# Another order of the steps in the six plans of an attention, gating and rotation kernel

## The chip, the core and the metric

The kernel runs on one core of one Trainium2 chip. The core has five engines with a queue each: TensorE (PE; its weight loads are shown as PEld), VectorE (DVE), ScalarE (ACT), GpSimd (POOL) and SyncE (SP, which only issues transfers). The metric is the device time of one execution in microseconds, and the number that stands for a kernel is the median of its runs.

## The reference

Three parts follow each other, all in fp32, for 8 batches of 576 positions: linear attention over 8 heads of 64, a gated block with a product over the positions, and a rotation block with two products over the positions.

```python
# attention: q, k, v are (8, 8, 576, 64)
q_s = softmax(q, axis=-1);  k_s = softmax(k, axis=2)
kv = np.einsum('bhsd,bhse->bhde', k_s, v)
x = heads_side_by_side(np.einsum('bhsd,bhde->bhse', q_s, kv))   # (8, 576, 512)
# gated block
h = np.maximum(x @ w_in, 0.0)                     # (8, 576, 1024)
u, v = h[..., :512], h[..., 512:]
v_n = (v - mean(v)) / np.sqrt(var(v) + 1e-06)
v_s = np.einsum('ts,bsd->btd', w_spatial, v_n) + b_spatial[None, :, None]
x = (u * v_s) @ w_out
# rotation block
theta = x @ w_theta
y = np.einsum('ts,bsd->btd', w_tok_r, x * np.cos(theta)) \
  + np.einsum('ts,bsd->btd', w_tok_i, x * np.sin(theta))
u = x + y
return u + np.maximum(u @ w_ch, 0.0)
```

## The kernel before

Every number is held as a high and a low part, and every product is three matmuls (high by high, high by low, low by high), so TensorE has most of the work. The kernel has two phases. Phase 1 goes through the batches and does the attention and the gated block; its results are written to DRAM. Phase 2 goes through the batches again and does the rotation block. The products over the positions in phase 2 are done with combined weights (seven products Q0 to Q6 for each batch, line 850), whose parts are made in phase 1.

The order of the work is written out by hand. A plan is a string of words; each word is one step (a function of some instructions), and the words are emitted from left to right within a manual schedule. Each engine issues its own instructions in the order of their emission and waits where an operand or a buffer isn't ready; between engines there is no order but that. So a plan sets the order on each queue, SP's and POOL's transfers among them, and which of the buffers in rotation a step gets. PSUM has three tiles of two banks and two of one bank in phase 1, two and four in phase 2; nine tiles of 128x576 ("t2") rotate in SBUF.

There are six plans. PLANS[0] (batch 0), PLANS[1] (batch 1), PLAN (batches 2 to 6) and LAST (batch 7) make phase 1; PLAN2 (batches 0 to 6) and LAST2 (batch 7) make phase 2. A word has a name, a number, flags (v: on VectorE, p: on GpSimd, c: on ScalarE; a, b: a part of the heads), and a stroke for work on the batch before.

- Attention, for the batch that comes next: ldk, ldq, ldv load (SP). kmax (VectorE, lines 373 to 381), kt (TensorE transposes, 388), kr (394), kbc (402), kmb (ScalarE, 407), ksub, kexp make the softmax of k, and K (446) the product with v, kn (459 to 467) its norm. qmax, qsub, qexp, qsum (501), qmul (509) make that of q; T (514) and t (525 to 528) turn it, X and x (528, 546) make the input of the gated block.
- Gated block: U (TensorE, line 187) and r (relu on ScalarE, 614); V (line 195), v (statistics, 567 to 578) and N (norm, 586 to 600); S (the product over positions, 187) and G (the gate, 629 on VectorE, 630 on ScalarE, 631 on VectorE or GpSimd); Y (187) and y (copy on ScalarE, 645, and a store).
- The weights come as 64-bit words and are converted on chip, 35 pieces in a fixed order, one for each pair of words B (first half: 242 to 264) and P (second half: 280 to 284); E makes sums for phase 2 (326 to 358). Plan 0 converts 18 pieces of w_in, w_sp and w_out while it runs the first batch.
- Phase 2, for the batch at hand: Q0 to Q6, with a (874), e (874), d (861), h (863), l (865) and s1, s4 operands late (f, F, g, G: 881, 883) between them; b loads the next operand (GpSimd, 674); C (line 195 or 187's helper) and o (905) make the output; in the last batch x does this by halves (917).
- Phase 2, for the batch that comes next: j, J (the input's high and low part, 687, 689), R (the remainder's parts, 707 and 708), m (theta, 195), w (730), t (737 to 742), r (749), y (757), z (764 to 772), s (787, 788), n (793, 794), p (798 to 802), i (807, 809), k (814, 817), I (821) and L (824). In LAST these stand with an H ahead of the word.

Of the kernel before, what the change touches and what calls it, by code (L numbers as in the profile page):

```python
# [1195 lines left out]
```

## Time and profile before

| | us |
|---|---|
| median of 3 runs | 1011.98 |
| lowest and highest | 1011.37 and 1012.64 |
| profiled execution | 1012.96 |
| its span in the trace | 1011.2 |
| TensorE busy | 948.7 |
| VectorE busy | 778.4 |
| ScalarE, GpSimd busy | 484.3 and 496.1 |

The profile's rows are of one execution. In a timeline row stand the start, the length, the engine, the line, the operation, the tiles written and read, the number of instructions, and in brackets the idle time before it with what ended it. The order of the rows on one engine is its order of issue. Phase 1 takes the first 587 us and phase 2 the rest; plan 0 takes the first 130, in which TensorE's granted clock is below full.

### The profile page before, as it was taken

To read this page: it belongs to the slowest core of one execution; us is meant where nothing else is said; L and a number is where in the kernel's file an instruction comes from. 1 tells how busy PE (TensorE), PEld (TensorE's weight loads), DVE (VectorE), ACT (ScalarE), POOL (GpSimd) and SP (SyncE) were. 2 spreads that over 40 slices of the span, in tenths; PEclk is the share of its full clock that TensorE was granted. 3 is DMA by queue.
4 is the path that set the end of the run, shared out by engine and by line. 5 is a ranking of instruction groups with operands and counts; after the bars stand their busy time and mean duration, and the time that the engine had idled before them with its cause. 6 is when DMAs were issued, how large, how long until landed. Compare 5 with 4: busy or idle time off the path is not lost.

```text
span 1011.2 us, 17199 instructions
## 1 busy us (share of the span) xinstructions
PE 948.7 (94%) x6816; PEld 893.8 (88%) x6816; DVE 778.4 (77%) x1140; ACT 484.3 (48%) x828; POOL 496.1 (49%) x496
## 2 busy tenths in 40 slices
PE   3588898999999999999999989999999999999997
PEld 2467888999899999999989989999999899999997
DVE  7887867877878778787424878988797988887863
ACT  3745446553555545545434645445353545454520
POOL 6366147554646566535202344646382637464460
PEclk9888899999999999999999999999999999999999
DMA  8542240516535365340132484544444262614332
GB/s 292 191 130 87 100 191 11 194 58 204 176 108 193 117 218 171 119 168 15 54 140 84 152 304 141 188 141 155 148 175 147 96 240 86 243 71 174 143 129 94
DMA packets 48064, 147.87 MB, mean 146 GB/s; under 512 B 8304, under 2 KB 21872, under 8 KB 38768
## 3 DMA queue, kind: packets, MB, share of 16 engines
q1 hardware_dynamic: 40464, 92.16, 26.0%
q0 software_dynamic: 7520, 54.63, 15.3%
q8 instruction: 53, 0.87, 0.4%
q14 instruction: 27, 0.22, 0.1%
HBM read 113.38 MB, written 33.39 MB: 145 GB/s over the span
## 4 chain that ended last, share of the span: by engine, by line
PE 46%; DVE 7%; POOL 5%; issue 2%; ACT 2%; DMA 1%; DVEq 0%; POOLq 0%; ACTq 0%
PE ps L850 18%; PE ps L187 14%; PE pb L195 9%; PE ps L195 3%; PE pb L757 1%; DVE t L787 1%; POOL s L793 1%; POOL w L807 1%; POOL s L794 1%; POOL w L814 1%; DVE t L764 1%; DVE w L814 1%; DVE t L741 1%; DVE t L765 1%; DMA sp<-op_w 1%
## 5 line engine op out<-in xcount | busy, mean ns | idle before, releaser
L187 PE MATMUL ps<-sp,vn 128*128 128x288 f32 x896 | 131.9, 306 | 9.6 <-DVE t L629 4.7
L187 PEld LDWEIGHTS ps<-sp,vn 128*128 128x128 f32 x896 | 125.5, 196 | 11.6 <-DVE t L629 4.9
L187 PE MATMUL ps<-g,wo 128*128 128x288 f32 x768 | 106.9, 297 | 1.7 <-ACT t L645 1.7
L187 PEld LDWEIGHTS ps<-g,wo 128*128 128x128 f32 x768 | 103.1, 189 | 2.8 <-ACT t L645 2.8
L187 PE MATMUL ps<-xh,w 128*128 128x288 f32 x512 | 95.1, 303 | 9.3 <-ACT w L280 7.7
L195 PE MATMUL ps<-w,xh 128*128 128x512 f32 x320 | 97.3, 397 | 3.4 <-ACT t L567 2.9
L187 PEld LDWEIGHTS ps<-xh,w 128*128 128x128 f32 x512 | 78.6, 193 | 11.3 <-ACT w L280 7.9
L187 PE MATMUL ps<-uh,wo 128*128 128x288 f32 x448 | 80.8, 296 | 0.0
L195 PE MATMUL pb<-w,xh 128*128 128x512 f32 x256 | 80.3, 395 | 0.0
L195 PEld LDWEIGHTS ps<-w,xh 128*128 128x128 f32 x320 | 59.2, 188 | 17.2 <-ACT t L567 3.5
L187 PEld LDWEIGHTS ps<-uh,wo 128*128 128x128 f32 x448 | 66.8, 188 | 0.9
L850 PE MATMUL ps<-sp,vn 128*128 128x288 f32 x360 | 60.4, 302 | 6.2 <-DVE t L772 4.0
L850 PEld LDWEIGHTS ps<-sp,vn 128*128 128x128 f32 x360 | 51.8, 192 | 7.8 <-ACT vn L802 4.2
L187 PE MATMUL ps<-xl,w 128*128 128x288 f32 x256 | 56.0, 301 | 0.0
L793 POOL TENSOR_TENSOR s<-t,t 128x256 f32<-128x256 f32 x30 | 23.8, 793 | 64.2 <-DVE t L788 64.2
L195 PEld LDWEIGHTS pb<-w,xh 128*128 128x128 f32 x256 | 46.8, 188 | 9.5
L730 ACT ACTIVATE t<-pb 128x512 f32<-128x512 f32 x36 | 21.5, 598 | 69.0 <-PE pb L195 57.9
L630 ACT CAST g<-t 128x576 fp32r<-128x576 f32 x32 | 21.5, 673 | 67.6 <-DVE t L629 67.5
L850 PE MATMUL ps<-sp,s 128*128 128x288 f32 x384 | 53.7, 295 | 0.0
L850 PEld LDWEIGHTS ps<-sp,s 128*128 128x128 f32 x384 | 52.4, 188 | 0.6
L850 PE MATMUL ps<-sp,w 128*128 128x288 f32 x288 | 48.9, 302 | 3.8 <-DVE w L814 3.3
L631 POOL TENSOR_TENSOR g<-t,g 128x576 fp32r<-128x576 f32 x17 | 25.2, 1485 | 52.2 <-ACT g L630 52.2
(251 smaller groups left out, 2502.2 us busy)
## 6 DMA issues: line engine op xcount, KB each, us to landing
sp<-op_t POOLq DMA_DIRECT2D x24, 1152.0 KB, 5.7
sp<-op_w POOLq DMA_DIRECT2D x16, 1152.0 KB, 5.4
vb<-in_v SPq DMA_DIRECT2D x8, 1300.0 KB, 7.6
y<-t SPq DMA_DIRECT2D x32, 288.0 KB, 2.2
qb<-in_q SPq DMA_DIRECT2D x7, 1152.0 KB, 5.5
out<-t SPq DMA_DIRECT2D x28, 288.0 KB, 2.2
kb<-in_k SPq DMA_DIRECT2D x6, 1152.0 KB, 5.1
st<-in_w_tok SPq DMA_DIRECT2D x9, 576.0 KB, 3.9
```

Source lines behind the costliest of these rows:

```text
L187: nc.tensor.matmul(out=ps[:, c, 0:CH], lhsT=a, rhs=w[:, c * CH:(c + 1) * CH], start=first and i == 0, stop=final and i == last,)
L195: nc.tensor.matmul(out=ps, lhsT=a, rhs=w, start=(i == 0), stop=(i == last))
L630: nc.scalar.copy(out=g_s[m], in_=g)
L631: eng.tensor_tensor(out=g_s[4 + m], in0=g, in1=f(g_s[m]), op=ALU.subtract)
L730: nc.scalar.activation(out=w, in_=ps, func=ACTF.Copy, scale=INV_2PI, bias=MAGIC)
L741: nc.vector.scalar_tensor_tensor(out=r, in0=w, scalar=-TWO_PI_LO, in1=r, op0=ALU.mult, op1=ALU.add)
L757: nc.tensor.transpose(yn[:, j * P:(j + 1) * P], y, ident)
L764: nc.vector.tensor_tensor(out=r, in0=r, in1=yn, op=ALU.mult)
L765: nc.vector.tensor_tensor(out=w, in0=w, in1=yn, op=ALU.mult)
L793: eng.tensor_tensor(out=th["s4"][:, t, :], in0=r[:, LO], in1=x, op=ALU.subtract)
L814: eng.tensor_tensor(out=z[1], in0=w, in1=f(z[0]), op=ALU.subtract)
L850: nc.tensor.matmul(out=ps[:, m, 0:CH], lhsT=a, rhs=x, start=i == 0, stop=i == len(pairs) - 1)
```

## The change

All six plans get another order of their words. Each plan keeps the same words with the same flags, so that each engine has the same instructions as before; nothing else in the kernel is changed. The words of B and P take the pieces in the same order as before, and each piece has its halves on the same engine.

```diff
--- before.py
+++ after.py
@@ -31,49 +31,50 @@
 ORDER = "u1 u0 u2 v3 u3 v2 v1 v0 s0 s3 s5 s2 s4 s1 o0 o2 o1 o3"
 LOADS = "ldk1 ldq1 ldv1 ldw2 ldw4"
 PLAN = (
-        "B0p V2 v2 qexp1 qsum1 qmul1 V1 v1 V0 v0 V4 v4 N2 N0 K1 kn1 U0 V3 r0 v3 N4v U2 r2 ldk2 N3cv N1 "
-        "U3 r3 P0 U1 r1 E0 T0 B t0 E1 S0 X0 G0 T1 P0v t1 S1 T2 S2 x0 kmax2 kt2 ldv2 t2 X1 G1 T3 ldq2 E0 "
-        "G2v x1 S3 kr2 G3v E1 kbc2 kmb2 Y0 t3p qmax2 y0 X2 x2 B0 Y1 qsub2 Y2 y1 X3 y2 Y3 ksub2v P0 x3 "
-        "kexp2 y3 E0v E1 "
-    )
+    "V1 V2 V4 v1 qexp1 V0 B0p K1 qsum1 qmul1 U2 V3 v2 v4 v0 U3 kn1 N0 N2 U0 v3 r2 U1 N4v N3cv "
+    "T0 r3 N1 r0 S0 r1 ldk2 P0 E0 T1 B t0 G0 X0 S1 T2 x0 E1 t1 kmax2 t2 S2 kt2 ldv2 G1 T3 P0v "
+    "G2v kr2 X1 x1 ldq2 E0 t3p S3 G3v kbc2 X2 E1 Y0 qmax2 Y1 y0 x2 y1 qsub2 kmb2 Y2 B0 ksub2v "
+    "y2 P0 X3 Y3 x3 y3 kexp2 E0v E1 "
+)
 PLANS = {
     0: (
-        "kmax1' kt1' kr1' kbc1' kmb1' qmax1a' qsub1a' qmax1b' qsub1bv' qexp1a' qexp1b' ksub1b' ksub1av' "
-        "qsum1a' qmul1a' kexp1a' K1a' kexp1b' K1b' qsum1b' ldk2' B0s' B0s' kn1a' qmul1b' T1' T2' T0' P' "
-        "t0' t1p' kn1b' T3' t2p' X0' x0' ldq1 t3' X1' x1' P' X2' X3' x2' x3' B U0 B0 ldv1 P0v P0v U1 r1 "
-        "B B B0p P0v U3 r0 B0 B0ps P0v P0 P0v B0s B0s kmax1 B0 P0 V0 kt1 v0 P0v U2 P V1 V4 kr1 r2 qmax1 "
-        "qsub1v B0 P N0cv B0p P P v1 kbc1 kmb1 ksub1 N1v V3 v3 v4 V2 v2 qexp1 N3 N2 N4 B0s qsum1 qmul1 "
-        "S1 kexp1 S0 G0 B0 G1 K1 kn1 B ldk2 S2 ldv2 G2 r3 kmax2 T0 t0 S3 kt2 P0v P G3v T1 t1p kr2 P0v "
-        "Y0 y0 X0 x0 T2 t2 kbc2 Y1 y1 B P0v T3 X2 Y2 X1 ldq2 x2 kmb2 y2 Y3 ksub2v t3 X3 x1p x3 qmax2 "
-        "qsub2 y3 "
+        "kmax1' qmax1a' kt1' qsub1a' kr1' qexp1a' kbc1' kmb1' qmax1b' qsub1bv' ksub1b' qexp1b' "
+        "qsum1a' qmul1a' ksub1av' qsum1b' kexp1a' K1a' qmul1b' kexp1b' T3' B0s' T1' B0s' K1b' T0' "
+        "kn1a' P' T2' t0' t1p' kn1b' t2p' X0' x0' t3' ldk2' X1' x1' X2' B B0 X3' P' x3' P0v x2' B "
+        "P0v P0v B U3 B0p B0 U0 P0v P0 r3 P0v U1 V0 r1 r0 kmax1 ldq1 B0ps P0 v0 qmax1 U2 V1 B0s "
+        "ldv1 P0v B0s N0cv V4 r2 B0 B0 V3 qsub1v P B0p P V2 v1 P P v4 v3 N1v kt1 v2 qexp1 N3 kr1 "
+        "N2 N4 kbc1 kmb1 qsum1 S0 ksub1 B0s S1 S2 kexp1 K1 qmul1 G0 T0 B0 G1 G2 kn1 T1 t0 ldk2 "
+        "kmax2 P0v S3 ldv2 B P G3v P0v kt2 t1p kr2 Y0 y0 X0 T2 x0 t2 Y1 X2 kbc2 B x2 X1 y1 T3 t3 "
+        "P0v kmb2 ksub2v Y2 ldq2 Y3 qmax2 y2 x1p X3 y3 qsub2 x3 "
     ),
     1: (
-        "V0 v0 kexp1 N0v V1 v1 V2 K1 qexp1 V3 kn1 v2 qsum1 qmul1 ldk2 U0 r0 V4 v3 U1 v4 r1 U2 T0 U3 B "
-        "N1 N2 N3 N4 t0p S0 r2 r3 B0p G0 T1 t1 ldv2 X0 S1 x0 X1 T2 G1 t2p kmax2 x1p S2 T3 ldq2 t3p kt2 "
-        "kr2 P E0 E1 P0v E0 E1 S3 X2 G2 G3v x2p kbc2 Y0 y0 B0s qmax2 Y1 Y2 y1 kmb2 P0v E0 E1 ksub2v "
-        "qsub2 y2 Y3 y3 X3 x3 kexp2 "
+        "V1 kexp1 V0 v1 V2 U1 v0 qexp1 v2 V4 N1 V3 qsum1 qmul1 K1 r1 N2 v4 U0 v3 kn1 r0 ldk2 B "
+        "N0v T0 t0p N4 U3 N3 r3 U2 ldv2 r2 S0 T1 X0 B0p P S1 G0 E0 x0 t1 kmax2 X1 S2 G1 x1p T2 T3 "
+        "kt2 ldq2 S3 t2p kr2 E1 X2 t3p G2 X3 G3v P0v Y0 qmax2 kbc2 Y2 x2p x3 Y1 y0 kmb2 E0 E1 y1 "
+        "y2 B0s qsub2 Y3 y3 ksub2v P0v kexp2 E0 E1 "
     ),
 }
 PLAN2 = (
-    "L1' L3' y4' Q0 f1 n3' f0 i2' I2v' R i3' I3' b0 z4' s4' p4' k4' I1' c j0 a0 Q1 Q2 j2 j1 J2 j3 "
-    "J3 b1 ldc f3 e0 g2 G2v g1 g3 G1v i4c' d0 y0 J1 f2 y1 h0 Q3 g0 G0v J0 m0 w0 G3 F3v e1 a2v Q4 t0 "
-    "r0 F0v m1 w1 e2 F2v F1 a1 z0 d1 l0v b2 a3v h1 t1c r1 s0 ldr Q5 d2 h2 l2v b3 n0 Q6 b4 d3 l1 m2 "
-    "n4' z1 s1 h3 l3 p0 k0p m3 L0p w2 t2c L4p' w3 t3c i1 C0 o0 i0c p1 k1p r2 C1 r3 y2 y3 C2 m4 I0 "
-    "o1 n1 z2 s2 C3 n2 z3 s3 p2 k2p o2 L2p w4 t4 o3 ldy p3 I4' r4 k3 "
+    "Q0 i2' L3' I1' i3' c y4' b0 I3' I2v' L1' f0 Q1 z4' p4' j1 k4' a0 j3 J1 Q2 e0 y0 n3' d0 "
+    "f2 g1 b1 j0 y1 g2 g0 G2v g3 R G1v Q3 n4' J3 b2 j2 J2 f3 J0 G3 h0 G0v m0 e1 a2v s4' ldc "
+    "w0 a1 t0 F2v m1 f1 w1 Q4 t1c a3v Q5 r1 e2 F1 l0v r0 F3v F0v d1 z0 s0 z1 Q6 h1 d2 m2 b3 "
+    "m3 l1 d3 p0 h3 h2 i4c' n0 y3 w2 s1 l3 p1 l2v L0p i0c y2 ldr t2c k0p n1 w3 b4 t3c C0 m4 "
+    "r2 C1 r3 o0 I0 C2 z2 s2 k1p o1 p2 z3 s3 p3 o2 C3 k3 n2 w4 t4 r4 k2p i1 o3 ldy L4p' L2p "
+    "I4' "
 )
 LAST2 = (
-    "L1' L3' y4' Q0 f1 n3' f0 i2' I2v' i3' I3' b0 z4' s4' p4' k4' I1' c a0 Q1 Q2 b1 f3 e0 g2 G2v g1 "
-    "g3 G1v i4c' d0 f2 h0 Q3 g0 G0v G3 F3v e1 a2v Q4 F0v e2 F2v F1 a1 d1 l0vv b2 a3v h1 Q5 d2 h2 "
-    "l2vv b3 Q6 b4 d3 l1v n4' h3 l3v L4p' I4' x0 x1 x2 x3 x4 x5 x6 x7 "
+    "i4c' I1' L1' i3' i2' Q0 I4' b0 L4p' f2 f1 s4' I3' L3' c Q1 a0 n3' I2v' y4' b1 f3 g1 G1v "
+    "f0 Q2 g3 G3 Q3 F2v e0 F0v F1 d0 g0 F3v h0 b2 l0vv k4' g2 G2v G0v e1 a2v Q4 e2 a1 d1 a3v "
+    "p4' Q5 Q6 d2 h1 z4' h2 l2vv d3 h3 l3v x2 l1v b3 x3 x1 x6 b4 x7 x0 x5 x4 n4' "
 )
 LAST = (
-        "ldy0 V2 v2 V0 v0 U1 N2v r1 V1 v1 N1v N0c V4 V3 v3 th U0 ldr v4 N4 B0 P0v B0s E0 E1v P E0 E1v "
-        "U2 r2 U3 ysp0 ysp1 N3c r3 B0p P0v ysp3 S0 ysp2 r0 S1 G0 Hm0 G1v Hy1 Hm1 Hw1 Ht1c Hw0 Ht0c S2 "
-        "rsp G2v Hr0 S3 ldy1 G3v Hm2 Hw2 Hm3 Hr1 E0 E1 Ht2 Hr2 Hy0 Hz0 Hs0 Hn0v Hp0 Hm4 Hy3 tok HL0 Hz1 "
-        "Hw3 Hs1 Y0 y0 Ht3 Hy2 Hz2 Hi0c Y2 Y3 Hk0p HI0v Hn1v Hp1 Hi1c Hk1p Hr3 Hw4 y2 HL1p Hs2 Hn2 Ht4c "
-        "Hp2 Hi2 Hr4 y3 HL2 Hz3 Y1 y1 Hs3 Hk2 HI2 Hy4 Hz4 Hn3 Hp3 HL3 Hs4 Hn4 Hi4 HI4v Hp4 HL4p Hi3 Hk3 "
-        "HI3v HI1v Hk4 "
-    )
+    "V0 V2 v2 V1 P0v v0 N2v V4 E0 N0c v1 E1v v4 V3 U1 v3 N4 ldy0 r1 N3c U2 N1v U0 S1 U3 r0 P "
+    "E0 G1v ldr B0 ysp2 th ysp1 S0 ysp3 rsp ysp0 Hm0 G0 Hw0 r2 E1v Hm1 Hm2 Ht0c Hw1 Hy0 S2 "
+    "Ht1c Hr0 S3 Hw2 Hy1 r3 Hy2 Hz0 Ht2 P0v Hm3 Hs0 Hr1 Hn0v Hr2 G2v G3v Hi0c Hp0 Hz1 Hk0p "
+    "Hw3 B0s Hm4 Hs1 Ht3 Hp1 E0 HI4v Hn1v HL1p Hz2 Hi4 Y0 Hi1c Hs2 HI1v Hr3 B0p Hp2 E1 Hw4 "
+    "tok Y2 ldy1 Hs4 Hi2 Hn2 Hy3 y0 HL0 Y1 HI0v Y3 Hy4 Hz3 Hs3 Ht4c Hp3 HI2 Hn4 y2 HL2 Hk2 "
+    "Hk3 Hr4 Hi3 Hn3 HL3 Hz4 Hp4 Hk4 y3 HL4p HI3v y1 Hk1p "
+)
 
 
 OPS = ("w11", "t2", "w21", "t3", "t1", "t4", "w22")
```

## Rows read from the trace of the kernel before

**Rows 1.** The page's first part, busy time of each engine, share, instructions.

```profile
PE 948.7 (94%) x6816; PEld 893.8 (88%) x6816; DVE 778.4 (77%) x1140; ACT 484.3 (48%) x828; POOL 496.1 (49%) x496
```

**Rows 2.** Busy time by stretch: length, PE PEld DVE ACT POOL, PEclk, DMA share, GB/s.

```profile
100.00:125.00 25.00, 20.34 (x137) 20.32 (x137) 21.31 (x34) 11.80 (x21) 5.65 (x4) 0.86 0.28 102
...
300.00:400.00 100.00, 97.80 (x730) 91.71 (x731) 81.32 (x111) 53.02 (x82) 59.10 (x52) 1.00 0.53 186
```

**Rows 3.** TensorE's waits by line: us in total, times, longest.

```profile
PE pb L388 <- DVE t L381: 10.7, 3, 7.8
PE ps L187 <- ACT w L280: 7.7, 1, 7.7
...
PE ps L187 <- DVE t L629: 4.7, 1, 4.7
PE ps L850 <- DVE t L772: 4.0, 1, 4.0
PE ps L850 <- DVE w L814: 3.3, 3, 1.1
...
PE ps L195 <- ACT t L567: 2.9, 2, 1.5
...
PE ps L187 <- ACT t L645: 1.7, 3, 0.8
PE ps L514 <- DVE qt L528: 1.6, 1, 1.6
PE ps L187 <- ACT u L614: 1.4, 3, 0.7
PE ps L850 <- DMA sp<-op_w: 1.2, 1, 1.2
...
PE ps L850 <- DVE kb L861: 0.8, 1, 0.8
```

**Rows 4.** Timeline of TensorE in plan 0: start, us, instruction, idle before.

```profile
50.27 0.85 PE L187 MATMUL ps<-xh,w 128*128 128x288 f32 x2 [7.69 <-ACT w L280]
...
76.05 0.73 PE L195 MATMUL ps<-w,xh 128*128 128x512 f32 x2 [1.39 <-ACT t L567]
...
104.69 6.69 PE L187 MATMUL ps<-sp,vn 128*128 128x288 f32 x28 [4.66 <-DVE t L629]
```

**Rows 5.** Timeline of TensorE in plan 2, its step Y3.

```profile
256.13 3.45 PE L187 MATMUL ps<-g,wo 128*128 128x288 f32 x24 [0.76 <-ACT t L645]
```

**Rows 6.** Timeline of DVE from 85 us: G2's start and kmax2.

```profile
103.88 0.75 DVE L629 TENSOR_TENSOR t<-ps,u 128x576 f32<-128x576 f32 x1
104.55 0.68 DVE L373 TENSOR_TENSOR t<-kb 128x512 f32<-128x512 f32 x1
105.27 1.99 DVE L376 TENSOR_TENSOR t<-t,kb 64x256 f32<-64x256 f32 x2
107.29 1.42 DVE L381 TENSOR_TENSOR t<-t,kb 128x512 f32<-128x512 f32 x2
```

**Rows 7.** The page's DMA issues, KB each, us to landing.

```profile
kb<-in_k SPq DMA_DIRECT2D x6, 1152.0 KB, 5.1
```

**Rows 8.** Line 284 on DVE: ns least, median, most; first and last start.

```profile
L284 DVE TENSOR_TENSOR st<-t,t x7: 692/759/1659, 178.5 to 486.7; 128x512 fp32r<-128x512 f32 x4, 128x576 fp32r<-128x576 f32 x3
```

**Rows 9.** Timeline of TensorE in phase 2, the border of a batch.

```profile
699.31 0.40 PE L850 MATMUL ps<-sp,w 128*128 128x288 f32 x1 [1.12 <-DVE w L814]
```

**Rows 10.** Timeline of DVE at the same border.

```profile
698.58 0.68 DVE L814 TENSOR_TENSOR w<-t,w 128x512 fp32r<-128x512 f32 x1
```

**Rows 11.** Line 708 (R's subtraction) on DVE: ns least, median, most.

```profile
L708 DVE TENSOR_TENSOR kvl<-yr,kvh x4: 684/3336/3358, 558.5 to 862.5; 128x512 fp32r<-128x512 f32 x4
```

**Rows 12.** Timeline of GpSimd in the last batch: a1 and b2.

```profile
982.76 2.00 POOL L874 TENSOR_TENSOR t<-t,kb 128x576 f32<-128x576 f32 x1 [6.71 <-DVE t L874]
984.71 0.57 POOL L674 DMA_DIRECT2D sp<-op_w  x1
```

**Rows 13.** Timeline of TensorE in the last batch: Q6.

```profile
990.29 1.04 PE L850 MATMUL ps<-sp,vn 128*128 128x288 f32 x6 [1.22 <-DMA sp<-op_w]
```

## The prediction

> **What bounds the kernel now.** I read the page's busy line first [rows 1]: TensorE is busy for 948.7 of 1011.2 us, so at most about 62 us can be won by any order, and only where TensorE stands still or runs on a low clock. The second view is busy time by stretch [rows 2]: in the 25 us from 100 on TensorE works 20.34 us at a granted clock of 0.86, while in the 100 us from 300 on it works 97.80 at clock 1.00. So plan 0 (all up to 130 us) has idle time and a half-clock part; the later plans have almost none. The third view is TensorE's waits by line [rows 3]. The reader is to see that the long ones happen once (7.8, 7.7, 4.7, 4.0 us), each in plan 0 or at the border of the phases, and that the short ones, up to 1.1 us, come at the borders of steps in the later plans. The engines issue in the order in which the plans' words are emitted, and nothing fixes the order of one engine against another. So a new order does two things only: it changes which instruction stands behind which on one queue, and when a buffer comes free.
>
> The profiled execution took 1012.96 us, 1.76 more than its span of 1011.2; the median of the runs is 1011.98, 0.98 below it. I make the sum on the span and carry its difference to the median. About 0.2%, 2.0 us, is what a measurement of this kernel can tell from no change.
>
> **Plan 0.** The instructions are the same, so only waits are added or removed.
>
> First products. Before, U0 and U1 run early, then TensorE waits 7.7 us for a converted piece of w_in, and U3 starts at 50.27 us [rows 4]. In the new order U3 comes first and needs the fifth converted piece; x3' and x2' (the last parts of x for batch 0) stand behind two more conversions on DVE. Counting DVE's instructions up to x2', I estimate the start of U3 at 46.5 us. The stretch before it gets emptier, so I take U3's 24 matmuls at the cold price. The row at 104.69 [rows 4] gives 6.69/28 = 0.239 us per matmul in a stretch where the clock is low; the row of a Y step on the warm clock [rows 5] gives 3.45/24 = 0.144, with its latency in it. U3 then ends at 52.2, U0 and U1 take 24 x 0.133 = 3.2 each (an estimate for back-to-back running, a little below the 0.144), and V0 starts near 58.6, against 50.27 + 24 x 0.239 = 56.0 before: +2.6 us.
>
> The Trainium skill (TensorE: Matmul & The Clock Gate, What's actually happening) says that the clock falls to 1.2 GHz after idling and comes back to 2.4 GHz only under sustained work. The rows agree in that the granted clock is below 1.00 just in the stretch with the waits [rows 2]; by the rule U0 would be cold too, and the plan 2.5 us longer than in my sum. The sum doesn't use it.
>
> V products. Before, V0 U2 V1 V4 V3 V2 have kt1 and kbc1 between them and stop for 2.9 us in two places for v statistics [rows 3]; the second stop ends at 76.05 [rows 4], from which V2 still has some 2.9 us to go, so it ends near 79. In the new order kt1 and kbc1 stand behind V2, and v0 and v1 have r1, r0 ahead of them but more products to hide behind. Five 12-matmul pieces of V, and U2, back to back need 16.4 us from 58.6, which gives 75.0; with some of the old cold stretch left I take 76. V2 ends 3 us earlier (0 to 4). The v chain up to S0 is the same in both and moves along.
>
> S3 and the second half. Before, S3 waits 4.7 us for G2 [rows 3], whose first instruction is issued at 103.88 [rows 6], behind kn1 and a whole conversion (B) on DVE. In the new order G2 stands directly behind G1, ahead of kn1 and that B: this wait goes, -4.7. What is late next is kmax2. It needs ldk2, which needs K1 to release kb; the landing takes 5.1 us [rows 7] and kmax2 0.68 + 1.99 + 1.42 = 4.1 [rows 6]. So kt2 can run 9.3 us behind K1. TensorE has T0, T1 and S3 between them (0.54 + 0.54 + 3.7 = 4.8, estimates at 0.133 per matmul for S3's 28) and waits about 4.7. G3v now stands behind kmax2 and a conversion's P0v, so Y0's last quarter is late by about 0.7 more. Before, kt2's wait cost about 1.4 (10.7 less the 7.8 at the very start, shared by two) [rows 3]. Net: +4.7 + 0.7 - 1.4 = +4.0. Bounds: +1 if ldk2 lands sooner than the row, +7 if G3v makes all of Y0 wait.
>
> Plan 0 in sum: -3.0 - 4.7 + 4.0 = -3.7, between -9 and +2.
>
> **Plans 1 to 6.** The rows give 1.7 us on y's copy (L645), 1.6 on qt (L528) and 1.4 on U's relu (L614) [rows 3]. In the new PLAN y1 stands before kmb2 and B0 on ACT and the r steps are spread, so 3.1 us go; of the 1.6 in plan 1 I keep half, a gain of 0.8. Against this, P0v now stands between G1 and G2v on DVE in five plans. Its multiplication alone takes 0.76 us at the median and up to 1.66 [rows 8], and S3 needs the PSUM tile that G reads. G2v's lateness is hidden by T3 and X1 in part; I take 0.2 us each, 1.0 in sum (0 to 7). Net -2.9, between -4 and +4.
>
> **LAST.** The head products still start when Hz4 is done, and the 4.0 us wait on L772 [rows 3] stays. Y1 waits about 1 for y0, which stands behind Hp2 and Hw4 on ACT; the gain of U before S balances it. Net 0, between -1 and +2.
>
> **PLAN2, seven batches.** Before, k3 (the low part, L814) is issued last of a batch, behind o3, and o3 waits for C3. At a batch's border Q0 therefore waits, as at 699.31 for 1.12 us [rows 9], where DVE does L814 only at 698.58, after o3 [rows 10]. In the list this is 3.3 us in three places [rows 3], and a weight load of Q0 waits in the others for about 0.4, so about 5.5 in all with what hangs on it. In the new order k3 stands ahead of n2, w4, t4 and o3, and this goes: -5.5. What comes in its place: d0 (which waits for the end of Q2) now stands ahead of G2v, R, G1v and J0 to J3 on DVE, and the J steps must be done before m0 reads them. Counting them at the 0.68 of a 128x512 subtraction [rows 10] the last J ends some 0.4 us ahead of m0. R's subtraction took 684 ns in one batch and 3336 in the median of four [rows 11]; with 3.3 us in R m0 waits 1.8 in each of the three or so batches that have it. And with m1 ahead of Q4, only Q5 covers e2, F1, d1 for Q6, again with about 0.4 us to spare. I take +1.5 for both, bounds 0 and +10. Net -4.0.
>
> The Trainium skill (SBUF — State Buffer, Who interferes with whom) says that a VectorE instruction with two SBUF inputs shares one read path with GpSimd and that the loser waits out the other's whole instruction. R is such an instruction and its spread of 684 to 3358 ns [rows 11] agrees; by the rule every J beside a running n or i step could be late in the same way, which is the rival below.
>
> **LAST2.** b2 (the load for Q6, L674) leaves GpSimd at 984.71, behind a1, which takes 2.00 us [rows 12]; Q6 then waits 1.22 us for it [rows 13]. In the new order b2 is ahead of a1: this wait goes, and the 0.8 on L861 [rows 3] is likely to go too, as e0 is freed of a0's contention. -2.0 (0 to -2.0). The tail's eight half products have another order and the same length: 0.
>
> **Sum.** -3.7 - 2.9 + 0 - 4.0 - 2.0 = -12.6 on the span: 1011.98 - 12.6 = 999.4. I forecast 1000.
>
> **The rivals.**
> (a) *Only part arrives.* The waits in plan 0 are limited by the conversions, of which there are as many as before, and kt2 and Y0 wait for all that S3 gains; the plans of phase 1 gain 1 and phase 2 about 5. Against it: G2 is plainly ahead of its old blockers. That is about 1006.
> (b) *DVE becomes the bound in phase 2: slower.* Place: between d0 and m0, and between e2 and Q6. If the subtractions of R, J and G are stretched as R's 3.3 us is [rows 11], m0 waits 2 to 2.5 and Q6 0.5 to 1 in each of 7 batches, about +21, less 5.5 at the borders; with P0v's stretch of about 0.9 in five PLANs, +4.5, and plan 0 and the last batch giving -6 to -12, the time is about 1020. It decides as soon as d0 to J0 take more than 0.4 us longer than counted.
> (c) *The orders cancel.* TensorE is at 97.80 of 100 us [rows 2] in most of the span; each wait is replaced by another as long: 1012.
> (d) *Plan 0 gains fully.* If V runs back to back and warm, and ldk2 lands before S3 ends, plan 0 gives -9 and not -3.7, and the borders' waits all go: about 991.
>
> **How the numbers follow.** The forecast (995 to 1004) has a chance of 0.42, (a) 0.18, (d) 0.13, (b) 0.20, (c) 0.07. The range must leave out no more than 0.2, so it reaches from the lower side of (d), 986, to the bulk of (b), 1018. Faster by over 0.2%: forecast, (a) and (d), 0.73. Within: 0.07. Slower: 0.20.
>
> **What would show it.** Plan 0: U3 first at about 46 us, no wait of S3 on L629, but one of kt2 on L381 of 4 to 5 us, and the first product of plan 1 about 4 us earlier. PLAN: waits on L645 and L614 gone, and perhaps one on L629 or on a PSUM tile before S3. PLAN2: no wait of Q0 on L814; waits on L687 (J) at m0 or on L861 at Q6 would show (b). LAST2: no wait on the load of op_w. The forecast fails if the new waits in one of the repeated plans are over 1 us per batch, since they come 5 or 7 times.

## The result and the profile after

The changed kernel takes 998.07 us (median of 4 runs, 996.75 to 998.78) against 1012.01 of the kernel before: a ratio of 0.9861, 95% interval 0.9844 to 0.9878. I had forecast 1000, between 986 and 1018. The profiled execution took 998.19 us with a span of 996.4, 14.8 less than before; the medians differ by 13.9, as the profiled execution of before was 1 us above its median. In its code every line below the plans has a number higher by one (L187 is now L188, L850 is L851).

The first part of the page, and then TensorE's waits by line (us in total, times, longest), to be read beside [rows 1] and [rows 3]:

```profile
PE 942.8 (95%) x6816; PEld 892.6 (90%) x6816; DVE 743.9 (75%) x1140; ACT 482.9 (48%) x828; POOL 483.2 (49%) x496
```

```profile
PE pb L389 <- DVE t L382: 12.1, 2, 7.6
PE ps L188 <- ACT w L281: 10.7, 1, 10.7
...
PE ps L851 <- ACT t L646: 6.2, 1, 6.2
PE ps L851 <- DVE s L825: 4.4, 3, 1.5
PE pb L403 <- DVE sm L395: 4.2, 2, 3.2
```

TensorE is listed as busy for 6 us less although it has the same 6816 matmuls: in the rows a matmul lasts about 0.30 us, while back to back one starts every 0.1325 us (288 columns, full clock), so some 0.16 us of each stall are listed as busy time and not as idle time. Of the waits of before, those on L629, L772, L814, L567 and L614, those of the Y steps on L645, and those on the load of op_w and on L861 are gone. The rows shown are new or longer: kt's (L382, of which 4.5 are kt2's in plan 0), U3's (L281, 10.7 for 7.7), the first Q0's on y's copy (L646, 6.2), Q1's on s2's low part (L825) and kbc1's (L395).

The best view for a change of order turned out to be the start of each plan's first product on TensorE. The difference of two such starts is the length of a stage, and the stages add up to the whole (us; from TensorE's timelines of both kernels; the last row is to the end of the span):

| stage | before | after | difference | forecast |
|---|---|---|---|---|
| plan 0 (to plan 1's first product) | 129.89 | 126.58 | -3.31 | -3.7 |
| plan 1 | 65.53 | 62.47 | -3.06 | -2.9 with the next |
| plans 2 to 6 | 318.64 | 311.54 | -7.10 | |
| LAST | 74.51 | 76.14 | +1.63 | 0 |
| PLAN2, seven batches | 377.28 | 377.00 | -0.28 | -4.0 |
| LAST2 | 45.35 | 42.67 | -2.68 | -2.0 |
| sum | 1011.20 | 996.40 | -14.80 | -12.6 |

So the sum was near and two of its terms were far off, in opposite directions: plans 1 to 6 gave three and a half times what I had put down, and PLAN2 gave almost nothing.

**Plan 0.** TensorE's timeline (start, length, instruction, idle before it), to be read beside [rows 4]:

```profile
46.31 0.85 PE L188 MATMUL ps<-xh,w 128*128 128x288 f32 x2 [10.67 <-ACT w L281]
...
78.81 0.65 PE L403 MATMUL pb<-turned,sm 128*128 128x128 f32 x4 [3.16 <-DVE sm L395]
...
96.63 3.96 PE L188 MATMUL ps<-sp,vn 128*128 128x288 f32 x28
105.12 1.12 PE L389 MATMUL pb<-turned,t 128*128 128x128 f32 x4 [4.53 <-DVE t L382]
105.89 5.26 PE L188 MATMUL ps<-g,wo 128*128 128x288 f32 x20
111.41 0.79 PE L188 MATMUL ps<-g,wo 128*128 128x288 f32 x4 [0.26 <-DVE g L632]
```

U3 is the first product and starts at 46.31; kt2 waits 4.53 us for kmax2; Y0's last quarter waits 0.26 for G3v. S3's wait of 4.7 us is gone. The half clock moved with the wait. Before, S3's 28 matmuls ran almost wholly at a granted clock of 0.50 (1.2 GHz) and took 0.239 us each [rows 4]; now they run at 1.00 and take 0.141. Instead Y0's first 20, behind kt2's wait, run almost wholly at 0.50 and take 0.263 us each.

**Plans 1 to 6.** Busy time by stretch (length, then busy us of PE, PEld, DVE, ACT, POOL, the granted clock, DMA share, GB/s), for batches 1 to 3 of the kernel before and of the changed one:

```profile
129.89:195.42 65.53, 62.91 (x495) 59.53 (x493) 50.23 (x69) 34.22 (x53) 37.75 (x32) 1.00 0.34 125
195.42:259.42 64.00, 63.18 (x495) 59.54 (x493) 49.85 (x74) 32.07 (x51) 31.30 (x30) 1.00 0.38 130
259.42:324.58 65.16, 63.51 (x495) 59.67 (x493) 53.53 (x78) 34.21 (x55) 39.38 (x36) 1.00 0.48 168
```

```profile
126.58:189.05 62.47, 62.47 (x495) 59.54 (x494) 43.52 (x71) 33.57 (x53) 35.49 (x33) 1.00 0.30 112
189.05:251.51 62.46, 62.46 (x494) 59.55 (x493) 45.23 (x70) 32.06 (x50) 28.76 (x28) 1.00 0.44 149
251.51:313.98 62.47, 62.47 (x495) 59.56 (x494) 49.50 (x79) 34.10 (x54) 38.38 (x36) 1.00 0.51 178
```

After, TensorE is busy in all of each stretch, and the stretch is the same 62.47 us each time; before, a batch had 0.8 to 2.6 us of idle time, and was besides listed as busy for 0.4 to 1.0 us more with the same instructions.

**The border of the phases, and phase 2.** TensorE's timeline at the first Q0, and at Q1 of batch 2:

```profile
576.73 1.81 PE L851 MATMUL ps<-sp,vn 128*128 128x288 f32 x6 [6.24 <-ACT t L646]
```

```profile
690.48 2.80 PE L851 MATMUL ps<-sp,s 128*128 128x288 f32 x19 [1.46 <-DVE s L825]
```

Behind the first wait stands ScalarE, which copies the last two outputs of phase 1 only after two casts that wait for Hz4 on VectorE:

```profile
573.55 0.62 ACT L803 CAST vn<-t 128x512 fp32r<-128x512 f32 x1 [1.50 <-DVE t L773]
574.98 0.62 ACT L803 CAST z_next<-t 128x512 fp32r<-128x512 f32 x1 [0.81 <-DVE t L773]
575.50 1.17 ACT L646 COPY t<-ps 128x576 f32<-128x576 f32 x2
```

Hz4 itself is not later. VectorE's row of it, before and then after, begins 71.46 and 71.55 us into LAST:

```profile
585.52 2.80 DVE L772 TENSOR_TENSOR t<-t,ps 64x512 f32<-64x512 f32 x4
```

```profile
572.14 2.80 DVE L773 TENSOR_TENSOR t<-t,ps 64x512 f32<-64x512 f32 x4 [0.21 <-issue]
```

Behind Q1's wait stands VectorE, where the second of two like subtractions (L825) takes 1.91 us and the first took 0.41; then GpSimd in the same time:

```profile
687.58 0.41 DVE L825 TENSOR_TENSOR s<-t,s 128x256 fp32r<-128x256 f32 x1
687.92 0.68 DVE L822 TENSOR_TENSOR w<-t,w 128x512 fp32r<-128x512 f32 x1
688.52 1.91 DVE L825 TENSOR_TENSOR s<-t,s 128x256 fp32r<-128x256 f32 x1
```

```profile
688.23 0.60 POOL L675 DMA_DIRECT2D sp<-op_t  x1 [3.49 <-PE ps L851]
688.86 1.27 POOL L822 TENSOR_TENSOR w<-t,w 128x512 fp32r<-128x512 f32 x1
```

**LAST2.** GpSimd's timeline, to be read beside [rows 12]: the load of Q6's operand now leaves ahead of a1, and Q6 doesn't wait [rows 13].

```profile
968.78 0.57 POOL L675 DMA_DIRECT2D sp<-op_w  x1 [3.30 <-PE ps L851]
969.77 1.99 POOL L875 TENSOR_TENSOR t<-t,kb 128x576 f32<-128x576 f32 x1 [0.42 <-DVE t L875]
```

### The profile page after: what moved, and what is told of

It is laid out like the page before. It is cut to its first block, busy times and chain, and to the rows that moved or that the text cites. A ratio compares the mean times of both kernels' runs of the same rounds, so it can differ in the third digit from the quotient of the medians.

```text
span 996.4 us, 17208 instructions
## 1 busy us (share of the span) xinstructions
PE 942.8 (95%) x6816; PEld 892.6 (90%) x6816; DVE 743.9 (75%) x1140; ACT 482.9 (48%) x828; POOL 483.2 (49%) x496
## 5 line engine op out<-in xcount | busy, mean ns | idle before, releaser
L188 PE MATMUL ps<-sp,vn 128*128 128x288 f32 x896 | 126.5, 299 | 0.0
L188 PEld LDWEIGHTS ps<-sp,vn 128*128 128x128 f32 x896 | 121.8, 191 | 0.2
L188 PE MATMUL ps<-g,wo 128*128 128x288 f32 x768 | 108.0, 300 | 0.3 <-DVE g L632 0.3
L188 PEld LDWEIGHTS ps<-g,wo 128*128 128x128 f32 x768 | 105.2, 192 | 1.0 <-DVE g L632 0.5
L188 PE MATMUL ps<-xh,w 128*128 128x288 f32 x512 | 94.7, 303 | 10.7 <-ACT w L281 10.7
L188 PEld LDWEIGHTS ps<-xh,w 128*128 128x128 f32 x512 | 78.5, 193 | 12.1 <-ACT w L281 10.9
L188 PE MATMUL ps<-uh,wo 128*128 128x288 f32 x448 | 80.0, 297 | 0.0
L851 PE MATMUL ps<-sp,vn 128*128 128x288 f32 x360 | 60.6, 303 | 6.2 <-ACT t L646 6.2
L188 PEld LDWEIGHTS ps<-uh,wo 128*128 128x128 f32 x448 | 66.0, 188 | 0.3
L851 PE MATMUL ps<-sp,s 128*128 128x288 f32 x384 | 54.8, 297 | 4.4 <-DVE s L825 4.4
L851 PEld LDWEIGHTS ps<-sp,vn 128*128 128x128 f32 x360 | 52.3, 193 | 7.3 <-ACT t L646 6.5
L851 PEld LDWEIGHTS ps<-sp,s 128*128 128x128 f32 x384 | 52.5, 188 | 5.7 <-DVE s L825 5.1
L575 DVE BATCH_NORM_STATS2 sm<-t 128x6 f32<-128x512 f32 (+1 forms) x40 | 27.2, 681 | 38.5 <-ACT t L568 33.0
L188 PE MATMUL ps<-xl,w 128*128 128x288 f32 x256 | 56.0, 301 | 0.0
L196 PE MATMUL pb<-w,xl 128*128 128x512 f32 x128 | 50.8, 397 | 0.0
L675 POOL DMA_DIRECT2D sp<-op_w x16 | 8.8, 552 | 86.2 <-PE ps L851 86.2
```

Of the source, the lines that this page charges most:

```text
L188: nc.tensor.matmul(out=ps[:, c, 0:CH], lhsT=a, rhs=w[:, c * CH:(c + 1) * CH], start=first and i == 0, stop=final and i == last,)
L196: nc.tensor.matmul(out=ps, lhsT=a, rhs=w, start=(i == 0), stop=(i == last))
L575: nc.vector.bn_stats(out=bs[0:n], in_=vr[0:n])
L675: nc.gpsimd.dma_start(out=op_buf[n % 2], in_=op_d[TURNS[n % len(TURNS)]])
L851: nc.tensor.matmul(out=ps[:, m, 0:CH], lhsT=a, rhs=x, start=i == 0, stop=i == len(pairs) - 1)
```

## The experiments

My theory was that the stages add and that each term has the mechanism that I had named. The rival was that stages feed each other, or that a removed wait is replaced by another one. All lengths of stages below are from TensorE's timeline of the run's profiled execution.

### Plan 0 alone

```diff
 PLANS = {
     0: (
-        "kmax1' kt1' kr1' kbc1' kmb1' qmax1a' ...
+        "kmax1' qmax1a' kt1' qsub1a' kr1' ...
```

> The kernel before with the new plan 0 alone. Theory A (the terms of the stages add, since each plan hands over the same state): plan 1 starts 3.3 us earlier, as in the changed kernel (126.58 against 129.89), TensorE waits 10.7 us for U3 and 4.5 us for kmax2's result, and the time is 1012.0 - 3.3 = 1008.7. Rival B (plan 0's new order also feeds plans 1 to 6, as its transfers and conversions end elsewhere): plans 1 to 6 change too, and the time is 1003 to 1006, or is within 1 us of before if the old plan 1 gives the 3.3 us back.

Measured: 1006.71 us, ratio 0.9953 (0.9939 to 0.9968), between the two theories' times. Plan 1 starts at 125.59, after U3's wait of 10.7 us and kt2's of 4.2. But plans 1 to 6 changed too: plan 1 takes 64.29 us instead of 65.53, plans 2 to 6 take 316.70 instead of 318.64, and waits of the old kind are still there (waits by line between 125 and 507 us):

```profile
PE pb L388 <- DVE t L381: 1.6, 1, 1.6
PE ps L514 <- DVE qt L528: 1.1, 1, 1.1
PE ps L187 <- ACT t L645: 0.8, 2, 0.6
```

So most of the gain is plan 0's, as theory A has it, and some 1.2 us come in plan 1, as rival B has it: of plan 1's two waits before, S0's on L525 (1.0 us) is gone and kt2's on L381 is still there. That this comes through the loads and conversions that plan 0 hands over is argued, not shown. The five later plans, identical in text to before, differ by 1.9 us in sum; in two other runs with the same old PLAN below they take 318.14 and 317.28, so more than 1 us of that is what these stalls vary from execution to execution.

### Plans 1 to 6 alone

```diff
 PLAN = (
-        "B0p V2 v2 qexp1 qsum1 qmul1 V1 v1 ...
+    "V1 V2 V4 v1 qexp1 V0 B0p K1 qsum1 ...
 ...
     1: (
-        "V0 v0 kexp1 N0v V1 v1 V2 K1 qexp1 ...
+        "V1 kexp1 V0 v1 V2 U1 v0 qexp1 v2 ...
```

> The kernel before with the new PLANS[1] and PLAN alone (batches 1 to 6). Theory A: these two plans carry their whole gain by themselves; every batch from 1 to 5 takes 62.5 us instead of 63.2 to 65.5, with no wait of TensorE over 0.3 us in them, and the time is 1012.0 - 10.2 = 1001.8. Rival B (part of that gain came from plan 0's new order, which leaves SP's loads and the conversions in another place): less than 7 us, over 1005.

Measured: 1004.76 us, ratio 0.9934 (0.9918 to 0.9951). Plan 1 takes 63.77 us, and plans 2 to 6 take 311.67: PLAN's whole gain of 7.0 us is its own. In plan 1, 1.8 of the 3.1 us are its own, and the other 1.3 are what the run before gave it; the two parts add. The time is 3 us over theory A's: besides plan 1's 1.3 us, plan 0 took 0.7 longer in the profiled execution and the seven batches of PLAN2, unchanged in text, 1.8 longer than in that of before (379.08 against 377.28), while LAST2 took 1.4 less. Rival B's gain below 7 us came (6.3 by the medians), its time over 1005 did not; its reason holds for plan 1 alone.

### One step of PLAN put back: y1

```diff
-... Y0 qmax2 Y1 y0 x2 y1 qsub2 kmb2 Y2 B0 ksub2v y2 P0 X3 Y3 ...
+... Y0 qmax2 Y1 y0 x2 qsub2 kmb2 Y2 B0 y1 ksub2v y2 P0 X3 Y3 ...
```

> The changed kernel with y1 behind qsub2, kmb2 and B0 in PLAN, about where the kernel before has it relative to these, and nothing else moved. Theory A (this place alone makes Y3 or X3 wait for Y1's PSUM tile, as in the kernel before): a wait on L646 of 0.5 to 0.8 us, 0.7 to 1.0 with its restart, in two to five of batches 2 to 6, and 998.1 + 3 = 1001 (1.5 to 5 more). Rival B (the waits went because the other steps gave ScalarE slack there, y1's place is not what counts): every batch stays at 62.5 us, 998.1.

Measured: 1001.95 us, ratio 0.9897 (0.9882 to 0.9913). The wait is back in three batches:

```profile
247.95 3.45 PE L188 MATMUL ps<-g,wo 128*128 128x288 f32 x24 [0.29 <-ACT t L646]
...
311.46 3.45 PE L188 MATMUL ps<-g,wo 128*128 128x288 f32 x24 [0.78 <-ACT t L646]
...
374.74 3.44 PE L188 MATMUL ps<-g,wo 128*128 128x288 f32 x24 [0.41 <-ACT t L646]
```

Plans 2 to 6 take 314.23 us instead of 311.54, 2.7 more, with 1.5 us of listed idle time. Theory A holds: the place of one copy on ScalarE is worth 2.7 of PLAN's 7.1 us. The intervals of this ratio and of the changed kernel's don't overlap. The time itself is 3.9 above that of the changed kernel, on another chip.

### k3 alone, in the kernel before

```diff
-"o1 n1 z2 s2 C3 n2 z3 s3 p2 k2p o2 L2p w4 t4 o3 ldy p3 I4' r4 k3 "
+"o1 n1 z2 s2 C3 n2 z3 s3 p2 p3 k2p o2 k3 L2p w4 t4 o3 ldy I4' r4 "
```

> The kernel before, with p3 and k3 moved ahead of o3 in PLAN2 and nothing else. Theory A (the wait of Q0 at the batch borders was worth what I put down, and the changed kernel lost it again to L1', which it had moved behind I2v'): with L1' still first, Q0's waits on the low part (1.31 us in each of three borders, 0.39 in the other three, restarts included) go and nothing replaces them: 1012.0 - 5.1 = 1006.9. Rival B (VectorE is so full at the border that whatever is served first makes another product wait): a new wait of about 1 to 1.5 us on another subtraction (s2's low part or I2v) at the borders and a time of 1010.5 to 1012.

Measured: 1012.48 us, ratio 1.0004 (0.9988 to 1.0019). Q0's wait on L814 is gone in all batches, and in the same three in which it had been 1.1 us Q2 now waits 1.44 to 1.49 for the copy c, which frees its PSUM tile:

```profile
704.48 1.07 PE L850 MATMUL ps<-g,vn 128*128 128x288 f32 x6 [1.44 <-ACT t L1032]
```

On ScalarE c (L1032) stands behind p4's two casts (L802), which wait for z4 on VectorE:

```profile
701.84 0.62 ACT L802 CAST vn<-t 128x512 fp32r<-128x512 f32 x1 [0.89 <-DVE t L772]
703.27 0.62 ACT L802 CAST z_next<-t 128x512 fp32r<-128x512 f32 x1 [0.81 <-DVE t L772]
703.79 0.63 ACT L1032 COPY t<-ps 128x576 f32<-128x576 f32 x1
```

The seven batches take 377.83 us instead of 377.28, and the time is that of before. Theory A falls and rival B holds, though in a place that neither named. What fits is that the border's work on VectorE is late as a whole, and whichever product needs a piece of it next waits.

### L1' first, in the changed kernel

```diff
-"Q0 i2' L3' I1' i3' c y4' b0 I3' I2v' L1' f0 Q1 ...
+"Q0 i2' L3' L1' I1' i3' c y4' b0 I3' I2v' f0 Q1 ...
```

> The changed kernel with L1' moved ahead of I1' and I2v' in PLAN2, so that VectorE makes s2's low part for Q1 before it makes I2v'. Theory A (L1' behind I2v' falls together with GpSimd's I1' and is stretched from 0.4 to 1.9 us, so Q1 waits 1.46 us, 1.70 with its restart, in three batches): the waits go, 998.1 - 5.1 = 993.0, and L1' takes about 0.4 to 0.8 us at its new place. Rival B (the wait moves to I2v', which is then the stretched one and holds Q2): 996.5 to 998, with a wait of Q2 on L822.

Measured: 998.01 us, ratio 0.9873 (0.9858 to 0.9888), which is not below the changed kernel's 0.9861. L1' is right as to its cause: both subtractions now take 0.75 us together, I2v' isn't stretched, and Q1 waits nowhere:

```profile
689.79 0.75 DVE L825 TENSOR_TENSOR s<-t,s 128x256 fp32r<-128x256 f32 x2
690.46 0.68 DVE L822 TENSOR_TENSOR w<-t,w 128x512 fp32r<-128x512 f32 x1
```

But the seven batches take 375.36 us, 1.6 less than in the changed kernel and not 5.1; with the same PLAN2 the last run below takes 377.57. A third limit comes up: a later product waits for its operand's load, up to 1.50 us in batch 2,

```profile
700.11 1.03 PE L851 MATMUL ps<-sp,vn 128*128 128x288 f32 x6 [1.50 <-DMA sp<-op_t]
```

which neither theory had. It is not new as such: with the changed PLAN2 as it is, three other runs have this wait, 0.2 to 1.0 us in batches 1 and 2. There, in batch 2, Q1's wait of 1.46 us comes first.

### Without the loads of the next batch

The kernel with L1' first, and without the loads ldy of PLAN2:

```diff
-... k2p i1 o3 ldy L4p' L2p "
+... k2p i1 o3 L4p' L2p "
```

> The kernel with L1' early (l1_first), with the loads ldy of PLAN2 left out, so batches from 2 on rotate old data of phase 2. It shows what the waits on the operand's load (0.41, 1.50 and 0.31 us on op_t in l1_first) are due to. Theory A (the load shares the DMA engines with ldy, 1152 KB issued just ahead of it): op_t lands in 5 to 6 us instead of 8.8, these waits are gone, and batches 1 to 6 of phase 2 take 1.5 to 2.5 us less in sum than in l1_first. Rival B (the load is late because it is issued late, when Q0 frees its buffer): it lands in 8 us or more also without ldy, and the waits stay.

Measured: one run, 994.24 us. No product behind the first Q0 waits, so the waits on op_t are gone, and batches 1 to 6 take 317.88 us instead of 321.89 with ldy. The DMA issues between 684 and 700 us (KB each, median us to landing), first with ldy, then without:

```profile
sp<-op_t POOLq DMA_DIRECT2D x2, 1152.0 KB, 8.8
```

```profile
sp<-op_t POOLq DMA_DIRECT2D x2, 1152.0 KB, 6.9
```

Theory A holds for the cause: the operand's load is late because ldy runs beside it, 8.8 us to landing with it and 6.9 without. Its numbers were off: 4.0 us are gained and not 1.5 to 2.5, and the landing falls to 6.9 us and not to 5 to 6. What the steps that read the loaded batch gain beside the operand's wait was not separated.

### k3 late, in the changed kernel

```diff
-... z3 s3 p3 o2 C3 k3 n2 w4 t4 r4 k2p i1 o3 ldy L4p' ...
+... z3 s3 p3 o2 C3 n2 w4 t4 r4 k2p i1 o3 ldy k3 L4p' ...
```

> The changed kernel with k3 behind o3 again in PLAN2, as in the kernel before. Theory A (k3's new place was worth nothing here, because three limits lie within 1.5 us of each other at the border: k3 for Q0, L1' for Q1, the operand's load for Q3): Q0 waits 1.1 us on L815 in batches 2, 4 and 6, Q1's 1.46 us on L825 shrinks by as much or goes, and batches 0 to 6 of phase 2 take the same within 1.5 us in sum. Rival B (k3's place is worth what I put down, and its gain was lost in another place of the batch): the sum rises by 4 to 5 us.

Measured: one run, 1000.20 us. Q0 waits again, 1.12 to 1.17 us in batches 2, 4 and 6 (the first is shown) and 0.6 in 1, 3 and 5:

```profile
687.55 0.40 PE L851 MATMUL ps<-sp,w 128*128 128x288 f32 x1 [1.17 <-DVE w L815]
```

Q1's wait is gone in exchange. The batches after a border with both limits (2, 4, 6) take 53.64 to 53.69 us, as in the changed kernel; those with only k3's limit (1, 3, 5) take 54.95 instead of 54.11 to 54.27. So k3's new place is worth some 2.4 us, all of it in the three batches in which no other limit lies close behind it; as batch 1 takes 54.27 to 55.27 in the runs with k3 early, the 1.7 us of batches 3 and 5 are the sure part. (The sum of all seven is 378.94 against 377.00; batch 0, which has no border ahead of it in phase 2, was 0.5 shorter here.) Theory A holds in its mechanism; its bound of 1.5 us is short.

### y1 and y3 early, in LAST

```diff
-"Hk3 Hr4 Hi3 Hn3 HL3 Hz4 Hp4 Hk4 y3 HL4p HI3v y1 Hk1p "
+"Hk3 y1 Hr4 y3 Hi3 Hn3 HL3 Hz4 Hp4 Hk4 HL4p HI3v Hk1p "
```

> The changed kernel with y1 moved ahead of Hr4 and y3 directly behind it in LAST, so that ScalarE copies the last two PSUM tiles of phase 1 before Hp4 (which waits for Hz4). Theory A (the 6.24 us wait of the first Q0 is these two copies, queued behind Hp4): Q0 then starts when Hz4 is done on VectorE at about 575.0 instead of 576.7, LAST takes 74.4 us instead of 76.1, the wait is about 4.5 us on L773, and the time is 998.1 - 1.7 = 996.4. Rival B (y3's copy ahead of Hr4's chain holds Hz4 by as much): LAST stays at 75.5 to 76.5 and the wait is on L773 at over 6 us.

Measured: 999.98 us, ratio 0.9877 (0.9855 to 0.9899). Q0's wait is now on Hz4 (L773), at 5.58 us; below it is VectorE's row of Hz4:

```profile
575.67 1.78 PE L851 MATMUL ps<-sp,vn 128*128 128x288 f32 x6 [5.58 <-DVE t L773]
```

```profile
572.61 2.80 DVE L773 TENSOR_TENSOR t<-t,ps 64x512 f32<-64x512 f32 x4 [1.07 <-issue]
```

LAST takes 75.48 us, where the other runs with this LAST take 76.14 to 76.39. Of 1.7 us expected 0.7 came: the copies did hold Q0, and once they are out of the way Hz4 holds it, which begins 72.42 us into the stage here (at 572.61, from 500.19) and 71.55 in the changed kernel (at 572.14, from 500.59), as Hr4's chain on ScalarE now stands behind a copy. Both theories have a part, and the time is not below the changed kernel's. With the LAST of before the stage took 74.49 to 74.51 in all five runs, also behind the new PLAN.

### G3 first, in plan 0

```diff
-"kmax2 P0v S3 ldv2 B P G3v P0v kt2 t1p kr2 Y0 y0 X0 T2 x0 t2 Y1 X2 ...
+"P0v S3 ldv2 B P G3v kmax2 P0v Y0 t1p y0 X0 T2 x0 t2 kt2 kr2 Y1 X2 ...
```

> The changed kernel with G3v ahead of kmax2 on VectorE and kt2 and kr2 behind X0 and T2 on TensorE in plan 0. Theory A (TensorE stands still for 4.5 us at kt2 because Y0 and X0 are queued behind kt2, which waits for ldk2 and kmax2; nothing else is late there): Y0 runs at once behind S3, the wait on L382 falls to under 2 us, plan 1 starts 3 to 4 us earlier, and batch 1 still takes 62.5 us: 998.1 - 3.5 = 994.6. Rival B (the chain of k for batch 2, from kmax2 to kexp2, is what sets the start of plan 1 or its K1, so a later kt2 gives the gain back): plan 0 ends earlier, but batch 1 takes 64 to 66 us, and the time is 997 to 999.

Measured: 999.74 us, ratio 0.9875 (0.9858 to 0.9893). kt2's wait falls to 2.09 us, but Y0, no longer covered by it, waits for G3 and for the converted pieces of w_out:

```profile
100.61 0.76 PE L188 MATMUL ps<-g,wo 128*128 128x288 f32 x4 [0.99 <-DVE wo L278]
...
105.42 0.53 PE L188 MATMUL ps<-g,wo 128*128 128x288 f32 x2 [1.57 <-ACT g L631]
...
110.42 0.66 PE L389 MATMUL pb<-turned,t 128*128 128x128 f32 x4 [2.09 <-DVE t L382]
```

Plan 1 starts at 125.78, against 125.54, 125.75 and 127.60 in the three kernels with the unmoved plan 0 on the same chip, and batch 1 takes 62.47 us. Neither theory: nothing is given back later, and the 3 to 4 us are not gained in the first place. Y0's four waits and kt2's are 5.2 us in sum, where the changed kernel has 4.8. What sets the end of plan 0 is then not the order in which TensorE asks for these results. That it is VectorE's list as a whole (kmax2, the conversions of w_out and the gates) fits the three waits, and was not tried further.

### b2 alone, in the kernel before

```diff
-... F2v F1 a1 d1 l0vv b2 a3v h1 Q5 ...
+... F2v F1 b2 a1 d1 l0vv a3v h1 Q5 ...
```

> The kernel before with b2 ahead of a1 in LAST2 and nothing else (d1's and l0's order to it unchanged on their engines). Theory A (Q6 waits for its operand because the load leaves GpSimd 2.0 us late behind a1): the load is issued about 2 us earlier, the 1.2 us wait of Q6 goes, and the last batch takes 1.2 to 1.4 us less (the stretch from its Q0 to the last product 39.0 to 40.2 us, where runs of the old order have 40.3 to 41.4). Rival B (a1 later makes d1 or l0 late): Q6 waits for L861 or L865 instead and the stretch stays.

Measured: one run, 1008.38 us. Q6 doesn't wait. From the last batch's Q0 to its last product it takes 39.01 us, as in the changed kernel (39.00); the old order takes 40.34 to 40.45 in three runs on another chip, and 41.37 in the profile of before, which alone has the further wait of 0.8 on L861. Theory A holds: b2's place is worth 1.3 to 1.4 us, and 2.4 where the wait on L861 is counted in, which this run doesn't have either.

### Both moves that helped

The changed kernel with L1' first and with y1 and y3 early, as in the two diffs above.

> The changed kernel with both moves that helped a stretch: L1' ahead of I1' and I2v' in PLAN2 and y1, y3 ahead of Hp4 in LAST. If the stretches add: LAST 75.5 instead of 76.1 (-0.7), batches 0 to 6 of phase 2 about 1.5 less, 998.1 - 2.2 = 995.9. If the earlier start of phase 2 only makes its loads later by comparison: 997 to 998.

Measured: 996.84 us (996.16 to 997.75), ratio 0.9854 (0.9835 to 0.9874), where the changed kernel had 0.9861 (0.9844 to 0.9878). Its LAST takes 75.45 us, as hoped, and its seven batches 377.57, which is not less: Q3's wait on the operand's load is 1.76 us in batch 2. What both runs with L1' first and ldy have is that batches 4 and 6 take 52.5 to 53.0 us, where the runs with the other order take 53.6 to 53.7; batch 2 takes 53.6 and 53.9. The intervals overlap in most of their length, so that it beats the changed kernel is not shown.

## Why the prediction was right, and where it was not

**Plan 0: right in its main steps.** U3 at 46.5 (46.31), V0 at 58.6 (58.76), V2's end at 76 (75.05, where kt1 follows), S3's wait gone, kt2's wait of 4.7 (4.53; 9.3 less 4.8 is 4.5 too), Y0's 0.7 (0.26), the sum -3.7 (-3.31). U0 took 3.39 us, so it ran at the full clock, and the 2.5 us that I set beside the sum did not come. Some of the agreement is luck. The 1.4 us that I credited for kt2's wait before were not there: that row's two short waits are kt1's in plan 0 (1.26) and kt2's in plan 1 (1.6). In kt2's new wait, ldk2 landed 1.1 us later than I had counted (6.2 for 5.1) and kmax2 was 1.1 shorter (3.0 for 4.1). Two waits I had not seen cancel: kbc1 stands still for 3.16 us, as kr1 is queued behind V's statistics on VectorE, and the first S product no longer stops in its course, where it had waited 2.7 and 0.6 us for V's norms (L595, L596). S3 at the full clock and Y0 at the half clock cancel too. And the stage varies by 2.8 us (last section); plan 1's first product starts at 126.4 in the mean of the eight executions with the new plan 0 and at 130.0 in that of the four with the old one, a gain of 3.7.

**Plans 1 to 6: the mechanism was right, the term was mis-sized.** I put down -2.9 and it gave -10.2. Three things were wrong in the step. I put the 1.6 us on qt (L528) into plan 1 and halved it; it is a wait of batch 4, in PLAN, as the first row below shows. Plan 1's own two waits, 1.6 us on L381 and 1.0 on L525, I left out. The new order takes all three away. I charged 1.0 us for P0v ahead of G2v, and no run with the new PLAN has a wait there of more than 0.4 us. And I took a stall at its listed idle time: as a matmul lasts 0.295 us in the rows and the next one could start after 0.1325, each stall costs 0.16 us more than is listed, and stalls below that are not listed as idle at all. This, with small delays behind the stalls, makes up the 0.4 to 1.0 us a batch by which TensorE was "busier" before. Of the 10.2 us, 7.0 were listed as idle and 3.2 were not. The removal itself is shown: the y1 run brings back 2.7 of it with one step, and the run with these plans alone keeps all of PLAN's. Which words took away the waits on L528 and L614 was not tried.

```profile
364.31 0.66 PE L514 MATMUL ps<-turned,qb 128*128 128x128 f32 x4 [1.56 <-DVE qt L528]
```

**LAST: the wait was right, its new cause was missed.** I wrote that Q0 still starts when Hz4 is done. Hz4 is done at the same place of the stage as before, but Q0 waits for y3's and y1's copies, which stand behind Hp4 and end 1.7 us after Hz4: +1.63. Y1's wait of 1 us for y0, which I had balanced against a gain, did not come.

**PLAN2: the step that failed is k3's -5.5.** The wait on L814 did go, but I took its going for a gain without asking what is late next. In the changed kernel that is L1' in batches 2, 4 and 6; with L1' first it is the operand's load, which lands later beside ldy; in the kernel before with k3 alone it is c. Three limits lie within 1.5 us of each other at a border, and taking away the first gives what lies between it and the second. The -0.28 is made up so, counted from Q0 to Q0: -2.1 in batches 1, 3 and 5, +1.3 in batches 2, 4 and 6, and +0.55 in batch 0. Of the first two, 1.05 us only moved across the border: three times y4's transposes (0.35 us), which stood ahead of Q0 and now stand behind it. Without them it is -1.05 where k3 was the only limit, and +0.2 where L1' takes back what k3 had cost. Batch 0's +0.55 is the clock's (last section). Rival (b)'s place, d0 to m0, showed nothing: there is no wait on L688 or on L862, so the +1.5 that I charged for it was not needed either. The sign of failure that I had named, a new wait of over 1 us in a repeated plan, did come with Q1's 1.46; it took PLAN2's gain and no more.

**LAST2: right, with some luck in the number.** -2.68 for -2.0, and b2 alone brings the stretch up to the last product to the same 39.0 us. But the wait on L861 (0.8) stands only in the profiled execution of before; in three other runs with the old LAST2 the stage took 43.96 to 44.31 us, 1.3 to 1.7 more than after.

The rival (d), with plan 0 gaining 9, is excluded by plan 0's -3.31 and the 4.5 us wait in it. That the forecast's total came out near is luck: 7 us too little in one term met 4 us too much in PLAN2 and 1.6 in LAST.

## What to carry to other kernels

Cost a new order by stages: the starts of each stage's first product in two traces show at once which term of a sum is off, and they repeat within 0.02 us where nothing stalls. Where a wait is to be removed, look up the next two things that the same and the following product need, and count as gain only the distance to the first of them. And where several short stalls all go, count each at its listed idle time and some 0.2 us more.

## What the hardware showed that I had not expected

**One subtraction, 0.41 or 1.91 us.** L825 with two operands in SBUF took 1.91 us while GpSimd issued a load and did a subtraction (L822, 1.27 us), and ended 0.3 us behind it; it did much the same in batches 4 and 6. Moved ahead, two of them took 0.75. The Trainium skill (SBUF — State Buffer, Who interferes with whom) has VectorE's second input and GpSimd share one path and the loser wait out the other's whole instruction. The trace agrees in that VectorE waits out GpSimd's subtraction, although VectorE's had begun 0.34 us ahead of it. So a step's place also decides its length, by what GpSimd does then.

**The clock behind the same stall.** After Q0's wait of 4.04 us the first 8.9 us of phase 2 ran at a mean granted clock of 0.81, and after the wait of 6.24 us the first 8.6 us at 0.73 (means of a part at 1.2 GHz and a part at 2.4). (Length, busy us of PE, PEld, DVE, ACT, POOL, clock, DMA share, GB/s; before, then after.)

```profile
588.57:597.50 8.93, 8.93 (x55) 8.93 (x56) 5.32 (x9) 4.97 (x13) 2.42 (x3) 0.81 0.95 348
```

```profile
576.73:585.31 8.58, 8.58 (x49) 8.58 (x49) 1.45 (x2) 2.94 (x7) 1.96 (x2) 0.73 0.63 203
```

It looks as if the longer stall had cost more, but the other runs show that it didn't. With plan 0 alone Q0 waited 4.02 us and the mean was 0.65; with k3 late it waited 6.49 us and the mean was 0.80:

```profile
581.07:589.82 8.75, 8.75 (x45) 8.75 (x46) 4.05 (x7) 3.67 (x8) 1.98 (x2) 0.65 0.86 296
```

```profile
576.76:585.51 8.75, 8.75 (x54) 8.75 (x55) 1.90 (x3) 3.66 (x10) 2.21 (x3) 0.80 0.69 223
```

What batch 0 takes follows this clock in all thirteen profiled executions. Over its first 8.75 us the mean is 0.84 where it takes 52.74 us, 0.79 to 0.81 at 52.90 to 53.12, 0.73 or 0.74 at 53.47 to 53.57, and 0.65 or 0.66 at 54.14 to 54.23. So the 0.55 us by which batch 0 is longer in the changed kernel go with the clock, and not with the new order as far as these runs show.

**Where executions differ.** With the same order plan 1's first product started between 125.36 and 128.18 in eight profiled executions, while batch 2 took 62.46 or 62.47 us in all of those with the new PLAN, but for the one with y1 moved. The seven batches of PLAN2, with the same text as before, took 376.86 to 379.14 us. Up to 1.5 of this is batch 0's clock; the rest is in the short waits of batches 1 and 5, such as Q3's on L874 (0.4 to 0.8 us in two runs, none in the others). So a small move in plan 0 or in PLAN2 can't be judged by the total.
